# A fused attention and MLP block: GpSimd's part of the late MLP moved to VectorE, gate vectors spread over eight steps, loads and early work reordered

## The chip, the cores and the metric

The kernel runs on one core of one Trainium2 chip. The metric is the device time of one execution in microseconds (us); lower is better. Engines: PE is TensorE, DVE is VectorE, ACT is ScalarE, POOL is GpSimd, SP issues most of the DMAs. "L509" is line 509 of the kernel's source; the same statement has a slightly different line number in the two kernels.

## The reference

```python
# x: 1 x 2048 x 640; k_cache, v_cache: 1 x 32 x 2048 x 128; bf16
mod = (_silu(c) @ w_mod).reshape(c.shape[0], 6, 1, -1)      # six vectors of 640
sa, ca, ga, sb, cb, gb = ...
h = _layernorm(x) * (1 + ca) + sa
x = x + ga * (softmax(h @ wq . K / sqrt(128)) . V) @ wo      # 32 heads, cache of 2048 keys
h = _layernorm(x) * (1 + cb) + sb
# MLP: g = gelu(layernorm(h) @ w1), its four column quarters shifted by +1, -1, +2, -2 rows
#      x1 = h + shifted(g) @ w2;  y = x1 + gelu(layernorm(x1) @ w3) @ w4
x = x + gb * y
```

## The kernel before

All work is written as operations with an engine, a duration estimate and a priority. A list scheduler in the kernel's own Python (`Plan`) fixes each engine's order when the kernel is built; on the chip each engine works strictly in that order. TensorE's order follows the priorities alone. So a changed estimate or priority moves instructions without changing what is computed.

The 2048 rows go in four chunks of 512. Attention is 128 "steps" (a head and a chunk), each with eight exps of 128x1024 on ACT. The "tail" after it holds, per chunk, w1 + GELU (A), w2 (B, by tiles of 128 rows), w3 + GELU (C), w4 (D, by tiles). The letter I stands for a chunk's layernorms before A, WO for the last output projection; `WOD`, `CH` and `I3D` shift the priorities of the last output projection's drains, of the work behind B and of I3. TensorE's order of these parts is a string:

```python
TAIL = ("A0 WO B0 B1 A1 B2 B3 A2 B4 B5 B6 I3 B7 C0 D0 D1 D2 D3 C1 A3 B8 B9 B10 B11 D4 D5 D6 B12 D7 ...")
...
def ln1(ch, prio):                       # layernorm of a chunk of x, then its transpose hT
    xs = ... load_x2(...)                # DMA
    for a in (0, 2):
        for i in (a, a + 1):
            ln_stats(xs[i].ap, (xs[i],), g, i, prio)           # DVE bn_stats, bn_aggr
        rstd_act(g, a, a + 2, prio - 100)                      # ACT: Ln, then Exp(-0.5 *)
        ...                                                    # DVE normalizes, DMA transposes, DVE scales
...
MS = 17                                  # gate vectors: 8 tiles of 5 matmuls, in two steps
for n, p in enumerate((2, 4, 3, 5)):
    ...
                 MM(HD), (s_bc, W12[n % 2]), (m,), NP * (MS + i // 20) + 3 + (i % 20) * 0.34 + 0.6, accum=True)
...
def mlp_in(ch, prio):
    eng = ("POOL", "DVE" if ch == 2 else "POOL") * 2           # layernorm, scale, shift, layernorm
    ...
def w2_tile(t, key):
    ...                                                        # DVE drains PSUM, statistics, rstd_dve (10 ops of 128x2)
    for u in (t - 1, t):
        v = xb[u]
        eng, late = ("POOL", 200) if t < SQ // 128 - 4 else ("DVE", 100)
        tt(eng, v.ap, v.ap, mod_t[5][:], ALU.mult, ...)        # 128x640 f32, POOL
        tt(eng, v.ap, v.ap, x1[u].ap, ALU.add, ...)
```

## Time and profile before

| | before |
|---|---|
| median of four runs | 1432.08 us (1431.37 to 1432.74) |
| profiled span | 1424.6 us (that run took 1430.3 us) |
| end of attention (first w1 matmul) | 1223.77 us |
| last matmul ends | 1420.04 us |

The first line to look at is who holds the chain that ended last (shares of the span by engine):

```profile
PE 92%; DVE 5%; SPq 1%; DMA 1%; issue 0%; ACT 0%; POOL 0%; POOLq 0%
```

TensorE's own work holds 92% of the chain; the other 8% lie with others, and DVE has the most of that. The next three fences are timelines (start, length, engine, line, operation, count, and in brackets the idle time before with what ended it). DVE near the start:

```profile
17.86 0.49 DVE L472 BATCH_NORM_STATS2 f_small<-f_xin 128x6 f32<-128x320 bf16 x1 [6.31 <-DMA f_xin<-in_A_x_dram]
18.27 0.53 DVE L552 TENSOR_SCALAR f_hT<-f_O,f_small 128x512 bf16<-128x512 bf16 x1
```

DVE stood 6.31 us in front of a statistics operation whose x was still under way, while the hT operation behind it could have run. The second place is in the tail; POOL, then TensorE:

```profile
1279.35 6.03 POOL L508 TENSOR_TENSOR f_y<-f_y,f_mod 128x640 f32<-128x640 f32 x4 [4.07 <-ACT f_y L515]
```

```profile
1295.11 5.17 PE L884 MATMUL f_M<-f_KV,f_OO 128*128 128x320 bf16 x22 [6.41 <-DVE f_wo L888]
```

While POOL works, TensorE waits 6.41 us for a DVE that is busy with tiny operations (the prediction shows these).

### The profile page before, as it was taken

Reading aid. Unit: us, or ns where it says so; the run is one execution under the profiler, and the core shown is the slowest. Engines: PE = TensorE matmul, PEld = TensorE weight load, DVE = VectorE, ACT = ScalarE, POOL = GpSimd, SP = SyncE. Lnnn points to the kernel's source line nnn. Section 1 sums busy time; section 2 is a strip of 40 time slices with the busy share of each in tenths; the row PEclk is TensorE's granted clock in tenths of the full one; section 3 lists DMA queues with packets and bytes.
Section 4 is the critical chain, followed back from the end, with each engine's and each line's share of the span. In section 5 each row is a group of like instructions: output and inputs, shape, how many; then the busy total and the mean of one; then the engine's idle time right before and its main releaser. Section 6 shows DMA issues by size and latency. Waiting matters only on the chain.

```text
span 1424.6 us, 29987 instructions
## 1 busy us (share of the span) xinstructions
PE 1388.6 (97%) x13176; PEld 940.9 (66%) x13176; DVE 544.4 (38%) x1349; ACT 1109.6 (78%) x1180; POOL 168.4 (12%) x132
## 2 busy tenths in 40 slices
PE   8899999999999999999999999999999999888998
PEld 6566767766676766666776666776766767544554
DVE  4353332233333233333223333323333355895662
ACT  4788868888888888888888888888888888752222
POOL 0000000000000000000000000001333366463300
PEclk9999999999999999999999999999999999999999
DMA  7661632142213321241215130512262123311110
GB/s 173 133 115 21 143 101 68 35 86 53 46 35 61 79 45 35 42 97 30 50 24 97 35 52 17 100 35 55 53 117 75 16 35 76 92 38 37 33 38 23
DMA packets 258963, 88.82 MB, mean 62 GB/s; under 512 B 236625, under 2 KB 257554, under 8 KB 258834
## 3 DMA queue, kind: packets, MB, share of 16 engines
q1 hardware_dynamic: 256210, 85.41, 29.6%
q8 instruction: 104, 1.70, 0.5%
q10 hardware_dynamic: 2624, 1.51, 0.5%
q14 instruction: 25, 0.20, 0.0%
HBM read 43.48 MB, written 2.62 MB: 32 GB/s over the span
## 4 chain that ended last, share of the span: by engine, by line
PE 92%; DVE 5%; SPq 1%; DMA 1%; issue 0%; ACT 0%; POOL 0%; POOLq 0%
PE f_O L726 32%; PE f_S L707 30%; PE f_M L638 10%; PE f_M L663 9%; PE f_M L884 2%; PE f_S L884 2%; PE f_S L871 2%; PE f_O L871 2%; DMA f_xin<-in_A_x_dram 1%; DVE f_small L472 1%; PE f_S L413 1%; PE f_M L844 1%; PE f_S L844 1%; DVE f_small L492 1%; DVE f_small L493 1%; DVE f_small L491 1%
## 5 line engine op out<-in xcount | busy, mean ns | idle before, releaser
L709 ACT ACTIVATE f_PQ<-f_S 128x1024 bf16<-128x1024 f32 x1024 | 1030.6, 1022 | 174.9 <-PE f_S L707 170.9
L726 PEld LDWEIGHTS f_O<-f_KV,f_PQ 128*128 128x128 bf16 x8192 | 539.8, 98 | 214.9 <-DVE f_OO L735 4.9
L726 PE MATMUL f_O<-f_KV,f_PQ 128*128 128x129 bf16 x8192 | 613.0, 220 | 3.5 <-DVE f_OO L735 3.4
L707 PE MATMUL f_S<-f_PQ,f_KV 128*128 128x512 bf16 x2048 | 609.4, 379 | 0.9 <-ACT f_PQ L709 0.9
L671 DVE TENSOR_TENSOR f_y<-f_M,f_y 128x320 f32<-128x320 f32 x192 | 94.4, 492 | 541.0 <-PE f_M L663 541.0
L663 PE MATMUL f_M<-f_wo,f_OO 128*128 128x320 bf16 x992 | 270.2, 299 | 1.3 <-DVE f_y L669 1.3
L508 POOL TENSOR_TENSOR f_y<-f_y,f_mod 128x640 f32<-128x640 f32 x56 | 87.5, 1577 | 1138.2 <-DVE f_y L671 1065.7
L707 PEld LDWEIGHTS f_S<-f_PQ,f_KV 128*128 128x128 bf16 x2048 | 192.5, 98 | 43.1 <-ACT f_PQ L709 1.9
L638 PE MATMUL f_M<-f_hT,f_wq 128*128 128x512 bf16 x640 | 161.3, 383 | 8.3 <-DVE f_hT L552 4.2
L638 PEld LDWEIGHTS f_M<-f_hT,f_wq 128*128 128x128 bf16 x640 | 62.5, 98 | 85.2 <-DVE f_hT L559 5.5
L663 PEld LDWEIGHTS f_M<-f_wo,f_OO 128*128 128x128 bf16 x992 | 94.8, 97 | 29.5 <-DVE f_y L669 1.8
L735 DVE TENSOR_TENSOR f_OO<-f_O,f_rl 128x256 bf16<-128x256 f32 x256 | 108.4, 423 | 8.3
L641 DVE CAST f_PQ<-f_M 128x512 bf16<-128x512 f32 x128 | 88.5, 691 | 53.6 <-PE f_M L638 53.4
L733 DVE RECIPROCAL f_rl<-f_O 128x2 f32<-128x2 f32 x256 | 43.4, 170 | 48.3 <-PE f_O L726 44.1
L884 PE MATMUL f_M<-f_KV,f_OO 128*128 128x320 bf16 x252 | 41.0, 310 | 9.0 <-DVE f_wo L888 7.9
L515 ACT ACTIVATE f_xn<-f_y,f_small 128x640 bf16<-128x640 f32 x12 | 10.8, 916 | 49.0 <-DVE f_small L497 47.1
L669 DVE COPY f_y<-f_M 128x320 f32<-128x320 f32 x32 | 15.7, 490 | 70.1 <-PE f_M L663 70.1
L884 PEld LDWEIGHTS f_M<-f_KV,f_OO 128*128 128x128 bf16 x252 | 23.9, 100 | 26.4 <-DVE f_wo L888 8.5
L874 ACT ACTIVATE f_OO<-f_O 128x512 bf16<-128x512 f32 (+1 forms) x28 | 16.6, 594 | 28.3 <-PE f_O L871 28.3
L874 ACT ACTIVATE f_OO<-f_S 128x512 bf16<-128x512 f32 (+1 forms) x28 | 16.6, 594 | 18.4 <-PE f_S L871 18.4
L472 DVE BATCH_NORM_STATS2 f_small<-f_y 128x6 f32<-128x320 f32 x64 | 29.4, 478 | 1.9 <-POOL f_y L508 1.8
L884 PE MATMUL f_S<-f_KV,f_OO 128*128 128x320 bf16 x196 | 30.0, 300 | 0.0
(118 smaller groups left out, 566.5 us busy)
## 6 DMA issues: line engine op xcount, KB each, us to landing
f_KV<-in_A_v_cache_dram SPq DMA_DIRECT2D x31, 512.0 KB, 4.7
f_wo<-in_A_wo_dram SPq DMA_DIRECT2D x8, 640.0 KB, 4.2
f_xin<-in_A_x_dram SPq DMA_DIRECT2D x15, 320.0 KB, 3.8
f_wq<-in_A_wq_dram SPq DMA_DIRECT2D x7, 640.0 KB, 4.5
f_W<-in_w_mod_dram SPq DMA_DIRECT2D x4, 800.0 KB, 4.8
out_dram<-f_xin SPq DMA_DIRECT2D x16, 160.0 KB, 1.8
f_KV<-in_B_w_dram SPq DMA_DIRECT2D x5, 432.0 KB, 3.3
f_KV<-in_A_k_cache_dram SPq DMA_TRANSPOSE x128, 2.7
```

The lines of the kernel that those rows point to most:

```text
L472: P.op("DVE", lambda e, hf=hf: e.bn_stats(s[:, hf * 6:hf * 6 + 6], src[:, hf * HD:(hf + 1) * HD]), 485, src_t, (s,), prio, slack=slack)
L508: P.op(eng, lambda e: e.tensor_tensor(out=out, in0=a, in1=b, op=op), COST[eng][0], rd, wr, prio, lat=300 if eng == "POOL" else None)
L638: P.op("PE", lambda e, i=i, kk=kk: e.matmul(m.ap, wq_t[g % 2][:, kk, hh * 128:(hh + 1) * 128], hT_t[ch][:, kk, :], start=(i == 0), stop=(i ...
L641: P.op("DVE", lambda e: e.tensor_copy(q.ap, m.ap), 690, (m,), (q,), s * NP - 90)
L663: P.op("PE", lambda e, m=m, qt=qt, hf=hf, hh=hh: e.matmul(m[:, 0:HD], OT_ap[gs][:, qt, hh, :], wo_t[g % 2][:, hh, hf * HD:(hf + 1) * HD], ...
L671: P.op("DVE", lambda e, m=m, yt=yt: e.tensor_tensor(out=yt.ap, in0=m[:, 0:HD], in1=yt.ap, op=ALU.add), 490, (m, yt), (yt,), s * NP - 60)
L707: P.op("PE", lambda e, sp=sp, r=r, kt=kt: e.matmul(sp[:, r * QC:(r + 1) * QC], K_ap[b][:, kt * 128:(kt + 1) * 128], q.ap, start=True, stop ...
L709: x = P.op("ACT", lambda e, sp=sp, pt=pt: e.activation(pt.ap.rearrange("p k q -> p (k q)"), sp.ap, ACT.Exp, scale=SCALE), 1021, (sp,), (pt ...
L726: ins = e.matmul(o[bk][:, w * 129:w * 129 + 129], pt[:, r, qt * 128:(qt + 1) * 128], V_ap[b][:, u, 0:129], start=(u == 0 and w == 0), stop ...
L735: evac.append(P.op("DVE", lambda e, ov=ov, i0=i0, bk=bk: e.tensor_tensor(out=On_ap[gs][:, 2 * bk:2 * bk + 2, hh, :], in0=ov[:, 0:258].rear ...
L871: P.op("PE", lambda e, m=m, f=f, kk=kk, fs=fs: e.matmul(m[0:fs, :], w3_ap[:, kk, f * 128:f * 128 + fs], nT_ap[ch][:, kk, :], start=(kk == ...
L884: P.op("PE", lambda e, f=f, hf=hf, fs=fs: e.matmul(m[:, hf * 512:hf * 512 + HD], gT_ap[0:fs, f, i * 128:(i + 1) * 128], w4_ap[f][0:fs, hf ...
```

## The change

Its intent: DVE and POOL no longer work at the same time in the MLP; reciprocal deviations in attention need no DVE; no engine stands in front of data that a DMA has yet to bring; the gate tiles fit into TensorE's slack.

```diff
-   u.ready = max(u.ready, (o.end if o in u.deps else o.start) + u.slack)
+   u.ready = max(u.ready, (...) + u.slack + (1500.0 if o.dma and u.eng in ("DVE", "ACT") and not u.dma else 0.0))
...
-   XP, XS = (0, -195, -20, -20), (0, -1, 22, 44)          # priority of the x loads
+   XP, XS = (0, -294, -20, -20), (0, -1, 22, 44)
-               ln_stats(xs[i].ap, (xs[i],), g, i, prio)
+               ln_stats(xs[i].ap, (xs[i],), g, i, prio, 0.0 if ch == 0 else 2000.0)
-               dmaT(... (raw[i],), prio)                  # transposes of a chunk
+               dmaT(... (raw[i],), prio - 400)
...                                                        # K, V and wq loads: other priorities
-   ... NP * (MS + i // 20) + 3 + (i % 20) * 0.34 + 0.6    # gate tiles: two steps
+   ... NP * (MS + i // KT) + 4 + i % KT + 0.65            # one tile in each of eight steps
...
-   WOD, CH, I3D = -50, -100, 50
+   WOD, CH, I3D = 0, -200, -200                           # and a new TAIL, which starts
+   # "A0 WO B0 B1 B2 A1 B3 A2 B4 B5 B6 B7 C0 I3 D0 D1 D2 D3 C1 A3 B8 ... D4 D5 D6 D7 B12 ..."
-   eng = ("POOL", "DVE" if ch == 2 else "POOL") * 2
+   eng = "DVE" if tail else "POOL"                        # POOL only for the first three chunks
-       shift(g, a, a + 2, prio)                           # DVE
+       negate(g, a, a + 2, prio, 1200.0)                  # ACT, in the first three chunks
-   (w2_tile: POOL multiply and add per tile)
+   (w4_tile: DVE adds w2's result to PSUM, multiplies by the gate, adds x1; last two tiles as before)
```

`rstd_dve` also loses one of its operations (the shift and the multiply become one). The 1500 and the 2000 are allowances in ns: the scheduler takes data that a DMA brings to be ready so much later (the 1500 for every DVE or ACT operation behind a DMA, the 2000 for the later chunks' statistics). POOL keeps the layernorms of the first three chunks; in the changed kernel its last operation ends at 1227.5 us, 21 us after the end of attention.

More of the change, by code (lines that the diff above doesn't have):

```diff
@@ L148, in schedule @@
                 u.ndep -= 1
-                u.ready = max(u.ready, (o.end if o in u.deps else o.start) + u.slack)
+                u.ready = max(u.ready, (o.end if o in u.deps else o.start) + u.slack + (1500.0 if o.dma and u.eng in ("DVE", "ACT") and not u.dma else 0.0))
                 if u.ndep == 0:
@@ L353, in fast_path @@
     xn = [T(t[:]) for t in xn_t]
-    tmp = [T(t[:]) for t in tmp_t] + [T(flat(wo_t[1])[:, i * 2 * D:(i + 1) * 2 * D].bitcast(F32)) for i in range(2)]
+    tmp = [T(t[:]) for t in tmp_t]
     rl = T(rl_t[:])
@@ L459, in fast_path @@
     nm = [T() for _ in range(NMV)]
-    nw = [[T(small(4)) for _ in range(4)] for _ in range(4)]
+    nw = [[T(small(4)) for _ in range(2)] for _ in range(4)]
     n_mv, n_nw = [0], [0]
@@ L481, in rstd_dve @@
         r = rs_ap[g][:, a:b]
-        v_, i_, t_, _u = nw[n_nw[0] % 4]
+        v_, t_ = nw[n_nw[0] % 4]
         n_nw[0] += 1
         n = b - a
-        v, it, t = v_[:, 0:n], i_[:, 0:n].bitcast(I32), t_[:, 0:n]
+        v, t = v_[:, 0:n], t_[:, 0:n]
         D_ = lambda f, rd, wr: P.op("DVE", f, 170, rd, wr, prio)
         D_(lambda e: e.tensor_scalar_add(out=v, in0=mv_ap[g][:, a:b, 1], scalar1=EPS), tuple(mvs[g][a:b]), (v_,))
-        D_(lambda e: e.tensor_scalar(out=it, in0=v.bitcast(I32), scalar1=1, scalar2=None, op0=ALU.logical_shift_right), (v_,), (i_,))
-        D_(lambda e: e.tensor_scalar(out=r.bitcast(I32), in0=it, scalar1=-1.0, scalar2=1595932665.0, op0=ALU.mult, op1=ALU.add), (i_,), (rs[g],))
+        D_(lambda e: e.tensor_scalar(out=r.bitcast(I32), in0=v.bitcast(I32), scalar1=-0.5, scalar2=1595932665.0, op0=ALU.mult, op1=ALU.add), (v_,), (rs[g],))
         for ca, cb in ((-0.703952253, 1.68191391), (-0.5, 1.5)):
@@ L498, in shift, with negate @@
                                                      op0=ALU.mult, op1=ALU.mult), 170, tuple(mvs[g][a:b]) + (rs[g],), (nm[g],), prio)
+    def negate(g, a, b, prio, slack):
+        P.op("ACT", lambda e: e.activation(nm_ap[g][:, a:b], mv_ap[g][:, a:b, 0], ACT.Copy, scale=-1.0), 220, tuple(mvs[g][a:b]), (nm[g],), prio, slack=slack)
     def normed(dst, dst_t, src, src_t, g, i, fp, prio):
@@ L503, in normed @@
              430 if fp else 240, (src_t, mvs[g][i], rs[g]), (dst_t,), prio)
-    COST = {"POOL": (1600, 1300), "DVE": (825, 430)}
+    COST = {"POOL": (1600, 950), "DVE": (825, 430)}
     def tt(eng, out, a, b, op, rd, wr, prio):
@@ L510, in scaled @@
     def scaled(eng, out, out_t, src, src_t, g, i, prio):
-        r, n = rs_ap[g][:, i:i + 1], nm_ap[g][:, i:i + 1]
-        rd = (src_t, rs[g], nm[g])
+        r, n, mu = rs_ap[g][:, i:i + 1], nm_ap[g][:, i:i + 1], mv_ap[g][:, i, 0:1]
         if eng == "ACT":
-            P.op("ACT", lambda e: e.activation(out, src, ACT.Identity, scale=r, bias=n), act(D), rd, (out_t,), prio)
-        else:
-            P.op(eng, lambda e: e.tensor_scalar(out=out, in0=src, scalar1=r, scalar2=n, op0=ALU.mult, op1=ALU.add), COST[eng][1], rd, (out_t,), prio,
-                 lat=300 if eng == "POOL" else None)
-    XP, XS = (0, -195, -20, -20), (0, -1, 22, 44)
+            P.op("ACT", lambda e: e.activation(out, src, ACT.Identity, scale=r, bias=n), act(D), (src_t, rs[g], nm[g]), (out_t,), prio)
+        elif eng == "POOL":
+            P.op("POOL", lambda e: e.tensor_scalar(out=out, in0=src, scalar1=n, scalar2=r, op0=ALU.add, op1=ALU.mult), COST[eng][1],
+                 (src_t, rs[g], nm[g]), (out_t,), prio, lat=300)
+        else:
+            P.op("DVE", lambda e: e.tensor_scalar(out=out, in0=src, scalar1=mu, scalar2=r, op0=ALU.subtract, op1=ALU.mult), COST[eng][1],
+                 (src_t, rs[g], mvs[g][i]), (out_t,), prio)
+    XP, XS = (0, -294, -20, -20), (0, -1, 22, 44)
     def ln1(ch, prio):
@@ L556, in ln1 @@
             for i in range(4):
-                dmaT(lambda e, i=i: e.dma_start_transpose(hT_t[ch][:, :, i * 128:(i + 1) * 128], xn[i].ap), 160, (xn[i],), (raw[i],), prio)
+                dmaT(lambda e, i=i: e.dma_start_transpose(hT_t[ch][:, :, i * 128:(i + 1) * 128], xn[i].ap), 160, (xn[i],), (raw[i],), prio - 400)
             for k in range(KT):
@@ L591, in load_head @@
         first = step_of(h // HG, 0, h % HG)
-        pr = (first - 12) * NP if h >= HG else -200 + 20 * h
-        n = max(0, first * NP - 12) if h < HG else (first - 12) * NP
+        pr = (first - 12) * NP if h >= HG else -310 + 20 * h
+        n = first * NP - 14 if h < HG else (first - 12) * NP
         load_k(h, pr, need=from_slot(n))
-        load_v(h, pr + 1, need=from_slot(n + 2))
+        load_v(h, pr + 1, need=from_slot(n + 1))
     def load_group(g):
@@ L600, in load_group @@
         load_wo(g, (step_of(g, 0, 0) - 2) * NP, from_slot((step_of(g, 0, 0) + 1) * NP + 12 * (g == 0)))
-    load_wq(0, 1, HG, -190)
+    load_wq(0, 1, HG, -295)
     for h in range(1, NKV):
@@ L611, in fast_path @@
         dma("SP", lambda e, n=n, p=p: e.dma_start(w_half[n % 2], w_mod[:, p * D:(p + 1) * D].rearrange("(k p) n -> p k n", p=128)),
-            800, (), (W12[n % 2],) + (tuple(wm) if n < 2 else ()), MS * NP - 30 + n, from_slot(MS * NP - 20 + 3 * n))
+            800, (), (W12[n % 2],) + (tuple(wm) if n < 2 else ()), MS * NP - 30 + n, from_slot((MS + 2 * n) * NP - 20))
         for hf in range(2):
@@ L618, in fast_path @@
                 P.op("PE", lambda e, m=m, sl=sl, k=k, n=n: e.matmul(m[:, 0:HD], s_bc[:, k, :], w_half[n % 2][:, k, sl], start=(k == 0), stop=(k == KT - 1)),
-                     MM(HD), (s_bc, W12[n % 2]), (m,), NP * (MS + i // 20) + 3 + (i % 20) * 0.34 + 0.6, accum=True)
+                     MM(HD), (s_bc, W12[n % 2]), (m,), NP * (MS + i // KT) + 4 + i % KT + 0.65, accum=True)
             P.op("DVE", lambda e, m=m, p=p, hf=hf: e.tensor_scalar_add(out=mod[p][hf].ap, in0=m[:, 0:HD], scalar1=1.0 if p == 4 else 0.0),
                  490, (m,), (mod[p][hf],), NP * MS - 60)
-    TAIL = ("A0 WO B0 B1 A1 B2 B3 A2 B4 B5 B6 I3 B7 C0 D0 D1 D2 D3 C1 A3 B8 B9 B10 B11 D4 D5 D6 B12 D7 B13 B14 C2 B15 "
+    TAIL = ("A0 WO B0 B1 B2 A1 B3 A2 B4 B5 B6 B7 C0 I3 D0 D1 D2 D3 C1 A3 B8 B9 B10 B11 D4 D5 D6 D7 B12 B13 B14 B15 C2 "
             "D8 D9 D10 D11 C3 D12 D13 D14 D15").split()
     WOKEY = 3000 + 50 * TAIL.index("WO")
-    WOD, CH, I3D = -50, -100, 50
+    WOD, CH, I3D = 0, -200, -200
     evac = []
@@ L676, in wo_group @@
                 if hf:
-                    tt("DVE" if last and qt % 2 else "POOL", x1[t].ap, w.ap, xb[t].ap, ALU.add, (w, xb[t]), (x1[t],) + tuple(hT[ch]), WOKEY + WOD if last else s * NP)
+                    tt("DVE" if last else "POOL", x1[t].ap, w.ap, xb[t].ap, ALU.add, (w, xb[t]), (x1[t],) + tuple(hT[ch]), WOKEY + WOD if last else s * NP)
                 if s == NS - 1 - HG and i == 7:
@@ L750, in rstd @@
                 rstd_dve(g, a, a + 2, prio)
+                shift(g, a, a + 2, prio)
             else:
                 rstd_act(g, a, a + 2, prio, 1200.0)
-            shift(g, a, a + 2, prio)
+                negate(g, a, a + 2, prio, 1200.0)
         for a in (0, 2):
@@ L762, in mlp_in @@
                 b = xb[t]
-                scaled("ACT" if tail else eng[i], b.ap, b, x1[t].ap, x1[t], g1, i, prio)
-                tt(eng[i], b.ap, b.ap, mod_t[4][:], ALU.mult, (b,) + tuple(mod[4]), (b,), prio)
-                tt(eng[i], b.ap, b.ap, mod_t[3][:], ALU.add, (b,) + tuple(mod[3]), (b,), prio)
+                scaled("ACT" if tail else eng, b.ap, b, x1[t].ap, x1[t], g1, i, prio)
+                tt(eng, b.ap, b.ap, mod_t[4][:], ALU.mult, (b,) + tuple(mod[4]), (b,), prio)
+                tt(eng, b.ap, b.ap, mod_t[3][:], ALU.add, (b,) + tuple(mod[3]), (b,), prio)
                 ln_stats(b.ap, (b,), g2, i, prio, 500.0)
@@ L769, in mlp_in @@
                 t = ch * 4 + i
-                scaled("ACT" if tail else eng[i], xn[i].ap, xn[i], xb[t].ap, xb[t], g2, i, prio)
+                scaled("ACT" if tail else eng, xn[i].ap, xn[i], xb[t].ap, xb[t], g2, i, prio)
                 dmaT(lambda e, i=i: e.dma_start_transpose(nT_ap[ch][:, :, i * 128:(i + 1) * 128], xn[i].ap), 160,
@@ L859, in w2_tile @@
                 dmaT(lambda e, j=j, z=z: e.dma_start_transpose(nT_ap[ch][:, :, j * 128:(j + 1) * 128], z.ap), 160, (z,), (nT[ch][j],), key + CH)
-            for u in (t - 1, t):
-                v = xb[u]
-                eng, late = ("POOL", 200) if t < SQ // 128 - 4 else ("DVE", 100)
-                tt(eng, v.ap, v.ap, mod_t[5][:], ALU.mult, (v,) + tuple(mod[5]), (v,), key + late)
-                tt(eng, v.ap, v.ap, x1[u].ap, ALU.add, (v, x1[u]), (v,), key + late)
+            if t == SQ // 128 - 1:
+                for v in (xb[t - 1], xb[t]):
+                    u = t - 1 if v is xb[t - 1] else t
+                    tt("DVE", v.ap, v.ap, mod_t[5][:], ALU.mult, (v,) + tuple(mod[5]), (v,), key + 100)
+                    tt("DVE", v.ap, v.ap, x1[u].ap, ALU.add, (v, x1[u]), (v,), key + 100)
     def w3_part(ch, key):
@@ L878, in w4_tile @@
         i = t % 4
-        w, b = tmp[2 + t % 2], xb[t]
+        b = xb[t]
         m = Tile(pool="W")
@@ L887, in w4_tile @@
         o_ = xin[t % 4]
-        P.op("DVE", lambda e: e.tensor_tensor(out=two(w.ap), in0=wide(m), in1=two(mod_t[5][:]), op=ALU.mult), 825, (m,) + tuple(mod[5]), (w,) + ((wo[1],) if t < 2 else ()), key - 1000)
-        P.op("DVE", lambda e: e.tensor_tensor(out=o_.ap, in0=w.ap, in1=b.ap, op=ALU.add), 825, (w, b), (o_,), key)
+        if t < SQ // 128 - 2:
+            P.op("DVE", lambda e: e.tensor_tensor(out=two(b.ap), in0=wide(m), in1=two(b.ap), op=ALU.add), 825, (m, b), (b,), key - 1000)
+            tt("DVE", b.ap, b.ap, mod_t[5][:], ALU.mult, (b,) + tuple(mod[5]), (b,), key)
+            tt("DVE", o_.ap, b.ap, x1[t].ap, ALU.add, (b, x1[t]), (o_,), key)
+        else:
+            w = tmp[t % 2]
+            P.op("DVE", lambda e: e.tensor_tensor(out=two(w.ap), in0=wide(m), in1=two(mod_t[5][:]), op=ALU.mult), 825, (m,) + tuple(mod[5]), (w,), key - 1000)
+            tt("DVE", o_.ap, w.ap, b.ap, ALU.add, (w, b), (o_,), key)
         dma("SP", lambda e: e.dma_start(out2d[t * 128:(t + 1) * 128, :], o_.ap), 160, (o_,), (), key)
```

## The prediction

> **What bounds the kernel now.** I read the page first (busy shares, then the chain of work that ended last), then a table of windows, then the list of waits of TensorE, then the timeline around each gap. The page's first part:
>
> ```profile
> PE 1388.6 (97%) x13176; PEld 940.9 (66%) x13176; DVE 544.4 (38%) x1349; ACT 1109.6 (78%) x1180; POOL 168.4 (12%) x132
> ```
>
> TensorE (PE) is busy for 97% of the 1424.6 us span and the chain puts 92% of the span on it, so little is to be had outside its gaps. The windows show where they lie; the columns are window and width, then PE, weight load, DVE, ACT and POOL busy, granted clock, DMA share, GB/s.
>
> ```profile
> 0.00:30.00 30.00, 24.12 (x313) 19.18 (x314) 14.49 (x44) 10.91 (x20) 1.15 (x12) 0.94 0.72 174
> 50.00:100.00 50.00, 44.83 (x434) 29.96 (x435) 26.07 (x77) 37.59 (x47) 0.00 (x0) 0.97 0.58 117
> 400.00:600.00 200.00, 200.00 (x2018) 140.23 (x2016) 60.73 (x149) 174.83 (x174) 0.00 (x0) 1.00 0.26 49
> 1250.00:1300.00 50.00, 39.18 (x202) 20.00 (x200) 47.68 (x113) 20.01 (x31) 35.05 (x24) 0.90 0.20 37
> ```
>
> The middle of attention is solid: one head step takes 9.26 us of matmuls (8.17 us without output projection, which is eight exps of 1022 ns). The gaps are at the start, before 100 us, and around 1250 to 1300 us, where DVE is 95% busy and POOL 70%. Part of "busy" at the start is dummy matmuls that keep the clock up. TensorE's waits:
>
> ```profile
> PE f_M L884 <- DVE f_wo L888: 7.9, 2, 6.4
> PE f_M L638 <- DVE f_hT L552: 4.2, 1, 4.2
> PE f_M L638 <- DVE f_hT L559: 4.0, 1, 4.0
> PE f_O L726 <- DVE f_OO L735: 3.4, 3, 1.7
> PE f_M L844 <- DVE f_y L847: 2.4, 1, 2.4
> PE f_M L618 <- DVE f_mod L620: 2.1, 4, 0.6
> ```
>
> All are waits on DVE. The longest is this stretch of DVE's timeline (start, length, operation):
>
> ```profile
> 1282.44 1.47 DVE L489 TENSOR_SCALAR f_small<-f_small 128x2 int32<-128x2 int32 x1
> 1283.94 1.45 DVE L491 SCALAR_TENSOR_TENSOR f_small<-f_small 128x2 f32<-128x2 f32 x1
> 1285.42 1.32 DVE L492 TENSOR_TENSOR f_small<-f_small 128x2 f32<-128x2 f32 x1
> ```
>
> These are reciprocal-square-root steps on 128x2 elements; at 1277 us the same lines take 0.16 us. POOL runs 1.5 us tensor_tensors back to back from 1279.35 to 1295.4: each small DVE operation lasts as long as one of them. Ten in a row hold the PSUM drain L888 back to 1294.25, and the matmuls of the third output tile start at 1295.11.
>
> **What the Trainium skill says.** "GPSIMD Engine Reference", section 8 Key points: GpSimd "Shares its SBUF interfaces with VectorE — contention with DVE instructions in a 2-port perf mode or with two SBUF inputs." The trace agrees, 1.3 to 1.5 us against 0.16. "TensorE: Matmul & The Clock Gate", What's actually happening: an idle array falls to half clock after about 3.4 us and needs such a time of work to recover. The trace agrees in kind: after the 6.41 us wait 28 matmuls take 6.09 us, not 4.29; after the 2.44 us wait ten take 2.73, not 1.52, so a shorter gap can do it too. "ScalarE: Activation LUTs", What ACT_TABLE_LOAD costs: about 1283 ns plus a drain of about 1380 per switch. The trace has 1283 ns; with the small operation between two loads a round trip took 1231.63 to 1236.86.
>
> **The change part by part.** TensorE's mathematics stays the same; what I count is its gaps, each in the coordinates of the trace before.
>
> *Start: +5.3 us.* DVE stands idle from 11.5 to 17.86 because the next chunk's statistics, which await a DMA, stand in front of the three operations that make the first hT. Their inputs, the transposes, are ready at 14.1 (ACT did its two at 14.14). In the new order those operations come first. DVE then makes hT at 14.14, 14.6 and 15.1 (0.45 apart); the projection ends near 16.1 with a warm array, the copy (0.69) at 16.8, scores, and the first exp at 17.5 instead of 22.77. The first K lands near 16.2 (last issue near 9, 7.2 to land), in time.
>
> *Second chunk: +4.8.* The wait at 48.4 cost 3.95 plus slow clock. The step from one projection's end (41.89) to the next (55.46) took 13.57 against 8.17, so 5.4, and the following one 0.5 more: 5.9. It came from the hT transposes standing behind K loads in SP's queue. They now come ahead. But DVE now awaits them before it drains the second head: x landing near 22.3, normalised near 28.7, transposes issued 27.4 to 32.6, last landing about 35.4 (4.1 each), five operations 1.7, to 37.1; TensorE wants that output bank at about 37.0 and gets its halves at 37.8 and 38.4. I leave 1.1 as a new stall.
>
> *Fourth chunk: +2.7.* At 80.5 to 92.4 a step took 11.84 against 9.26, because statistics awaiting x stood before drains. The new order puts them behind the projection copy, and x is asked for earlier relative to use.
>
> *Gate vectors: +3.1.* Two steps took 13.56 each, 8.6 over normal, of which 40 matmuls of 0.135 are 5.4; the rest is waiting for a PSUM bank. One tile in each of eight steps gives 8 x 0.68, the same 5.4, and a whole step to drain.
>
> *Tail: +15.2 on paper.* From 1223.77 to 1420.0 is 196.3 us. The work in it is 20 x 1.08 (w1) + 4.3 (last output projection) + 16 x 1.36 (w2) + 56 x 1.08 (w3) + 16 x 4.22 (w4) = 175.5. So 20.8 are gaps and slow clock, plus 2.8 just before. POOL is out of the MLP; DVE gets 14 x 3 + 2 x 4 = 50 tile operations of 0.82 instead of 16 x 2 + 4 x 2 = 40, 8 us more over the tail, but loses some 26 us of stretched small ones. Walking the new order by hand:
> - Attention ends at 1222.0, 1.7 earlier (no 4.1 us pair of contended DVE operations before the drains).
> - ACT now switches tables twice in the tail, seven loads there (with the GELU's first) against four: 3 x 1.28 = 3.9 us, and the first trip lies inside the GELUs of the first w1 part. With four PSUM tiles TensorE stands from 1227.4 to 1230.75; the output projection ends at 1235.9, as before (1235.7).
> - The second trip delays the next GELUs; the w2 tile that needs them starts at 1247.5, against 1245.7.
> - Then the 2.44 wait shrinks to 0.4, w3 starts at 1260.2 against 1262.2, the w4 tiles at 1275.5 against 1278.5.
> - From there DVE has slack (drain of the first w4 tile at 1280, needed 1284.2), so the 6.41 + 1.8, the 1.53 and the small ACT waits vanish. 129.2 us of matmuls end at 1404.8 against 1420.0.
>
> From the 15.2 I take 2.0 for half clock after the two new waits on ACT (3.3 and 2.0 us) and 2.5 for waits my hand walk misses, leaving 10.7. The moved negation adds 12 ACT operations of 0.2 us inside ACT's slack of 1.08 us per step: nothing.
>
> Sum: 5.3 + 4.8 + 2.7 + 3.1 + 10.7 = 26.6, and 1431.9 - 26.6 = 1405.3. The deduction is the doubtful part: without the 2.5 it would be 1402.8. I put the point between, at 1404.
>
> **Rivals.**
> 1. *ACT's table switches take the place of the POOL contention.* For: three more loads, in front of GELUs that TensorE needs at once, while DVE waits in order behind POOL results that themselves await ACT. Against: it is one stretch of 25 us and later work has slack. If each trip costs 4 us more than my walk says, about 1412.
> 2. *DVE becomes the bound after 1250.* For: 50 tile operations and all statistics on one engine, 95% busy there before. Against: that business is mostly stretched waiting; each w4 tile gives DVE 4.22 us for three operations (2.5). If w4 tiles wait 1 us on average for half of them, 1412.
> 3. *The reordered loads only move the stall.* DMA is at 0.9 from 3 to 18 us, and three more K transposes go before x. If x lands at 25 instead of 22.3, the second query copy and the second head's drain are late by 2 to 3 us each: 1408.
> 4. *Everything hides.* Neither new stall nor half clock: 15.2 in the tail, 1.1 back at the second chunk: 1431.9 - 32.2 = 1399.7.
>
> **Range and chances.** Faster by 2% means below 1403.2, right beside my point. The surest parts (start 5.3, gates 3.1, the 6.41 us wait with its slow clock 8.2) make 16.6 us, so 1415 is a pessimistic end and I set 1413; the low end is below rival 4 by some 3 us. Slower would need a new wait of 55 us: hardly. Faster by over 2% 0.46, within 0.53, slower 0.01.
>
> **What would show it right or wrong.** First exp near 17.5; no wait of TensorE for hT of several us before 60 us; eight steps near 9.94 us around 190 to 260 us and no wait for f_mod; no 128x2 DVE operation above 0.5 us after POOL's last operation near 1233; seven table loads in the tail, a wait of TensorE on ACT of about 3 us some 5 us after attention's end; at most 0.5 us of waits per w4 tile. It is wrong if TensorE still waits several us on DVE after 1250 us with POOL silent, or if a head step in mid attention is not 9.26 us.

## The result, and the profile after

| | before | after |
|---|---|---|
| median | 1432.08 us | 1400.81 us (1400.64 to 1401.11) |
| ratio of fast runs | | 0.9782 (95%: 0.9765 to 0.9799) |
| profiled span | 1424.6 us | 1395.0 us |

A ratio is the mean time of one kernel's fast runs over that of the other's of the same rounds, so it is not quite the ratio of the medians quoted. All runs compared here are in the fast state. The changed kernel is faster by 2.2%. The profiled run of before was 1.8 us quicker than its median, so the traces explain 29.6 of the 31.3 us.

The page's busy line and its chain line, after:

```profile
PE 1380.7 (99%) x13176; PEld 939.8 (67%) x13176; DVE 518.0 (37%) x1337; ACT 1114.6 (80%) x1195; POOL 123.5 (9%) x106
```

```profile
PE 96%; ACT 2%; POOL 1%; DVE 0%; DMA 0%; issue 0%; ACTq 0%; POOLq 0%
```

The matmuls are the same; DVE's 5% of the chain became 0, ACT has 2% now. The windows that the prediction showed (columns as there):

```profile
0.00:30.00 30.00, 26.01 (x344) 20.39 (x345) 15.85 (x48) 14.18 (x23) 1.15 (x12) 1.00 1.03 219
50.00:100.00 50.00, 50.00 (x506) 34.71 (x503) 25.54 (x75) 45.18 (x53) 0.00 (x0) 1.00 0.58 109
1250.00:1300.00 50.00, 50.00 (x269) 25.34 (x268) 23.16 (x71) 26.04 (x42) 0.00 (x0) 1.00 0.17 40
```

TensorE fills both later windows. In the last one DVE went from 47.68 to 23.16 us busy although it has more full-size operations to do over the tail (78 of 128x640 with two inputs after the end of attention, 59 before): much of the rest had been waiting. TensorE's waits, all of 1 us and more:

```profile
PE f_S L668 <- ACT f_PQ L836: 3.2, 1, 3.2
PE f_S L712 <- ACT f_PQ L714: 2.7, 3, 1.8
PE f_S L850 <- ACT f_PQ L836: 1.7, 1, 1.7
PE f_S L413 <- POOL f_ones L381: 1.0, 1, 1.0
```

No wait for DVE above 0.3 us is left. The first and the third are new: TensorE waits for GELUs (L836) in the tail. The second has a piece at the start. ACT, then TensorE:

```profile
24.34 0.20 ACT L477 ACTIVATE f_small<-f_small 128x2 f32<-128x2 f32 x1 [2.03 <-DVE f_small L473]
```

```profile
25.50 0.60 PE L712 MATMUL f_S<-f_PQ,f_KV 128*128 128x512 bf16 x2 [1.83 <-ACT f_PQ L714]
```

ACT stood before an Ln whose statistics DVE could not finish before the second chunk's x had landed (20.9 us), and the exps behind the Ln, which TensorE needed, stood with it.

Where the 29.6 us came from, by the starts of the query projections (one per step) in both traces:

| stretch | before | after | gained |
|---|---|---|---|
| to the third projection | 32.47 | 29.04 | 3.4 |
| to the sixth (second chunk's first stall lies between) | 63.09 | 53.56 | 9.5, 6.1 more |
| to the ninth (fourth chunk) | 92.36 | 80.51 | 11.8, 2.3 more |
| to the twenty-eighth (gate tiles) | 276.90 | 261.90 | 15.0, 3.2 more |
| to the end of attention | 1223.77 | 1206.27 | 17.5, 2.5 more |
| from there to the end of the last matmul | 196.3 | 184.2 | 12.0 more |

Between the twenty-eighth and the 118th projection nothing changed (15.0 at both ends). The last 2.5 us of attention were two waits of TensorE for DVE (1.66 and 0.90 us at 1217 and 1218 us), which are gone.

### The profile page after: what moved, and what is told of

It reads as the page before. It is cut to its first block, busy times and chain, and to the rows that moved or that the text cites. A ratio compares the mean times of both kernels' runs of the same rounds, so it can differ in the third digit from the quotient of the medians.

```text
span 1395.0 us, 29964 instructions
## 1 busy us (share of the span) xinstructions
PE 1380.7 (99%) x13176; PEld 939.8 (67%) x13176; DVE 518.0 (37%) x1337; ACT 1114.6 (80%) x1195; POOL 123.5 (9%) x106
## 3 DMA queue, kind: packets, MB, share of 16 engines
q10 hardware_dynamic: 2624, 1.51, 0.5%
## 4 chain that ended last, share of the span: by engine, by line
PE 96%; ACT 2%; POOL 1%; DVE 0%; DMA 0%; issue 0%; ACTq 0%; POOLq 0%
PE f_O L731 33%; PE f_S L712 31%; PE f_M L643 10%; PE f_M L668 10%; PE f_S L890 2%; PE f_M L890 2%; PE f_S L877 2%; PE f_O L877 2%; ACT f_PQ L836 1%; PE f_S L413 1%; PE f_S L850 1%; PE f_M L850 1%; POOL f_y L511 0%; PE f_S L832 0%; PE f_M L623 0%; DMA f_xin<-in_A_x_dram 0%
## 5 line engine op out<-in xcount | busy, mean ns | idle before, releaser
L511 POOL TENSOR_TENSOR f_y<-f_y,f_mod 128x640 f32<-128x640 f32 x40 | 61.3, 1542 | 1058.2 <-DVE f_y L676 1050.8
L890 PE MATMUL f_S<-f_KV,f_OO 128*128 128x320 bf16 x224 | 34.3, 300 | 0.0
L890 PE MATMUL f_M<-f_KV,f_OO 128*128 128x320 bf16 x224 | 34.3, 300 | 0.0
L472 DVE BATCH_NORM_STATS2 f_small<-f_y 128x6 f32<-128x320 f32 x64 | 29.3, 478 | 10.7 <-POOL f_y L511 10.7
L890 PEld LDWEIGHTS f_M<-f_KV,f_OO 128*128 128x128 bf16 x224 | 20.6, 97 | 14.0 <-issue 5.5
L890 PEld LDWEIGHTS f_S<-f_KV,f_OO 128*128 128x128 bf16 x224 | 20.5, 97 | 13.3 <-issue 4.2
```

The source lines that it names most:

```text
L511: P.op(eng, lambda e: e.tensor_tensor(out=out, in0=a, in1=b, op=op), COST[eng][0], rd, wr, prio, lat=300 if eng == "POOL" else None)
L890: P.op("PE", lambda e, f=f, hf=hf, fs=fs: e.matmul(m[:, hf * 512:hf * 512 + HD], gT_ap[0:fs, f, i * 128:(i + 1) * 128], w4_ap[f][0:fs, hf ...
```

## The experiments

Twelve kernels ran. The first three do one part of the change alone, on the kernel before.

**Gate vectors alone** (b_gates): the two gate lines of the diff, nothing else.

> The kernel before with only the gate vectors spread, one tile in each of eight steps. Theory (the parts of the gain are separate and add up): eight steps of 9.94 us take the place of two of 13.56 us and six of 9.26 us, so 3.1 to 3.2 us less than before, about 1428.9 us, and no wait of TensorE for the gate tile. Rival (the steps saved are given back in the attention that follows, because the exponentials set its pace): 1431 to 1432 us.

Measured: 1428.58 us against 1431.72 us, ratio 0.998 (0.9972 to 0.9987). The steps are 9.94 us long and the wait for the gate tile is gone. 3.1 us, as the theory has it.

**Loads and allowances alone** (b_loads): the lines of the diff down to the loads.

> The kernel before with only the reordered loads and the two allowances for data that arrives by DMA. Theory (all that was gained in the first nine steps comes from here): the start of the ninth step (the step after the eighth chunk-head pair) moves from 92.4 to 80.5 us and stays so to the end, about 1420 us. Rival (part of the early gain comes from VectorE having less to do, which is in the other part): 1423 us or more.

Measured: 1419.01 us against 1431.72, ratio 0.9912 (0.9894 to 0.993). The ninth projection starts at 80.39 us. 12.7 us: the last projection starts 12.0 us earlier than before (1192.89 us for 1204.87). The theory holds for the first nine steps, but "stays so to the end" hides two things that cancel in part. The last step of attention became about 1.5 us longer (the granted clock was 0.50 from 1207.54 to 1210.95 us). And the tail became about 3.2 us shorter, 193.1 us for 196.3: in this run DVE's order in the tail differs from that of the kernel before, and TensorE's waits fell elsewhere. (The first matmul of the tail has no record in this trace; its start is worked out from the matmul before it.)

**MLP part alone** (b_mlp): all the rest of the diff.

> The kernel before with only the MLP part: its elementwise work on VectorE and ScalarE, the shorter chain of small operations, the new order of the tail. Theory (the parts add up): the last step of the attention 2.7 us shorter and the tail 12.1 us shorter, so about 14.8 us less in the profile and 1415 to 1418 us. Rival (the tail gained because it found other clock or other loads than before): 1420 us or more, with waits for VectorE left in the tail.

Measured: 1415.90 us against 1431.72, ratio 0.9889 (0.9872 to 0.9906). TensorE's waits in it:

```profile
PE f_M L643 <- DVE f_hT L557: 4.7, 1, 4.7
PE f_M L643 <- DVE f_hT L564: 4.4, 1, 4.4
PE f_S L668 <- ACT f_PQ L836: 3.2, 1, 3.2
```

The two early waits for hT are those of the kernel before; the tail is that of the changed kernel, with its new wait for a GELU. 3.1 + 12.7 + 15.8 = 31.6 us, and the whole change gained 31.3. The parts add up, though they are not wholly separate, since the loads' part moves the tail by some us.

**The allowances taken out again** (a_noslack): in the changed kernel, without the 1500 and the 2000.

```diff
-   ... + u.slack + (1500.0 if o.dma and u.eng in ("DVE", "ACT") and not u.dma else 0.0))
+   ... + u.slack)
-               ln_stats(xs[i].ap, (xs[i],), g, i, prio, 0.0 if ch == 0 else 2000.0)
+               ln_stats(xs[i].ap, (xs[i],), g, i, prio)
```

> The changed kernel with the two allowances for data that arrives by DMA taken out again; priorities and order of the loads stay. VectorE then has the second chunk's statistics, whose x landed at 20.9 us, ahead of the drain of the first head's queries (15.75 us in the changed kernel). Theory (the early start comes from these allowances): the first scores come at about 22.5 us in place of 16.5 us, the later steps as in the changed kernel, and the time is 1404 to 1407 us. Rival (the order of the loads alone makes the early start): 1400 to 1402 us.

Measured: 1408.92 us, ratio to before 0.984: 8.1 us more than the changed kernel, above the range of the theory.

```profile
22.82 1.89 PE L712 MATMUL f_S<-f_PQ,f_KV 128*128 128x512 bf16 x4 [6.09 <-DVE f_PQ L646]
```

The first scores come at 22.82 us, as expected. What the theory missed: the eighth step took 11.23 us again in place of 9.26 (projections at 78.02 and 89.25), so the fourth chunk's gain came from the allowances too, about 2 us. The second chunk's stall did not come back (8.18 us from the fourth to the fifth projection): that one was cured by the order of the loads.

**Needless GpSimd work in the tail** (a_noise). Nobody reads its result; the other engines' order is the same.

```diff
+    for n in range(44):
+        P.op("POOL", lambda e: e.tensor_tensor(out=mod_t[2][:], in0=mod_t[2][:], in1=mod_t[3][:], op=ALU.add), ...)
```

> The changed kernel with 44 needless GpSimd additions of 128x640 after GpSimd's last useful instruction, some 68 us of them, read by nobody; the instruction order of the other engines is the same. Theory (GpSimd beside VectorE costs, whatever GpSimd computes): the 128x2 operations of VectorE in that stretch rise from 0.15 us to about 1.3 us each, TensorE waits for VectorE again, and the time is 1406 to 1415 us. Rival (the tail gained by the new order and the shorter chain alone): under 1403 us, small operations still under 0.3 us.

Measured: 1436.51 us, ratio 1.0024 (1.0014 to 1.0033): all of the gain and 4 us more are lost. This is DVE in the window 1231 to 1290 us, grouped by line and form (busy time and mean ns behind the bar), first in the changed kernel, then with the needless work:

```profile
L511 DVE TENSOR_TENSOR f_y<-f_y,f_mod 128x640 f32<-128x640 f32 x12 | 9.6, 818 | 0.0
L491 DVE TENSOR_TENSOR f_small<-f_small 128x2 f32<-128x2 f32 x15 | 2.1, 155 | 0.0
L472 DVE BATCH_NORM_STATS2 f_small<-f_y 128x6 f32<-128x320 f32 x18 | 8.2, 478 | 0.0
L853 DVE TENSOR_TENSOR f_y<-f_S,f_y 128x640 f32<-128x640 f32 x3 | 2.5, 825 | 1.5 <-PE f_S L850 1.4
```

```profile
L491 DVE TENSOR_TENSOR f_small<-f_small 128x2 f32<-128x2 f32 x9 | 10.3, 1150 | 0.0
L511 DVE TENSOR_TENSOR f_y<-f_y,f_mod 128x640 f32<-128x640 f32 x4 | 7.1, 1778 | 0.0
L472 DVE BATCH_NORM_STATS2 f_small<-f_y 128x6 f32<-128x320 f32 x14 | 6.5, 474 | 0.0
L853 DVE TENSOR_TENSOR f_y<-f_S,f_y 128x640 f32<-128x640 f32 x3 | 2.4, 810 | 0.2 <-PE f_S L850 0.2
```

The orders of TensorE, DVE and ACT are the same in both traces. A 128x2 multiplication goes from 155 to 1150 ns, a 128x640 one from 818 to 1778. Statistics (one source) and the drain of a PSUM tile (L853: one source in PSUM, one in SBUF) do not change. Operations `tensor_scalar` with one source are held too: of 128x2 from 163 to 990 ns (L487) and, on integers, from 158 to 582 (L488), of 128x640 from 607 to 1154 (L522). The Trainium skill, "SBUF — State Buffer", section Who interferes with whom, says just this: a VectorE instruction with two SBUF inputs contends with a GpSimd instruction that reads SBUF, the winner holds the shared port for its whole instruction, and the other fully blocks; one SBUF input outside the 2-port modes does not contend. The trace agrees, line by line; for `tensor_scalar` the page leaves the 2-port modes as the reason, which no run here shows by itself. TensorE's longest wait is then

```profile
PE f_M L850 <- DVE f_y L853: 14.4, 1, 14.4
```

because the drain, itself not slowed, stands behind slowed operations. The theory's mechanism holds; its size (5 to 14 us) was far too small for 76 us of unbroken GpSimd work.

**The same time of GpSimd in shorter instructions** (a_noise_ts): 78 operations `tensor_scalar` (one source) in place of the 44 additions.

> As the run with 44 needless GpSimd additions, but 78 GpSimd operations of one source (tensor by two scalars, 128x640, 0.87 us each), about the same 68 us of GpSimd. Theory (a VectorE instruction that meets a GpSimd instruction ends when that one ends, whatever its form): small operations of 0.4 to 0.9 us in place of 0.15, and 1410 to 1425 us. Rival (only GpSimd instructions with two sources hold VectorE): small operations of 0.15 us and under 1403 us.

Measured: 1409.78 us, ratio 0.9846 (0.9831 to 0.9861).

```profile
L491 DVE TENSOR_TENSOR f_small<-f_small 128x2 f32<-128x2 f32 x14 | 6.8, 503 | 0.0
```

GpSimd was busy for 72.6 us here against 75.8 us in the run before, 0.93 us per instruction against 1.72, and the loss is 9.0 us against 35.7. A GpSimd instruction with one source also holds VectorE; the time fell just short of the theory's range. The loss fell fourfold for instructions little more than half as long, which no proportion explains; the two runs differ in form as well as in length, so what share each has is not settled.

**The old order of the tail** (a_oldorder): the changed kernel with `TAIL` and `WOD, CH, I3D` of the kernel before.

> The changed kernel with the order of the tail and the three priorities of the kernel before; engines and chain as in the changed kernel. Theory (taking GpSimd out of the MLP is what gains, not the order): 1400 to 1404 us. Rival (the order does most of it): 1408 us or more.

Measured: 1407.64 us, ratio 0.9833 (0.9818 to 0.9848): 6.8 us more, near the rival. The theory as I had put it falls. The traces show why. TensorE, then ACT:

```profile
1235.28 1.87 PE L850 MATMUL f_S<-f_W,f_PQ 128*128 128x320 bf16 x10 [4.31 <-ACT f_PQ L836]
```

```profile
1225.95 1.28 ACT L477 ACT_TABLE_LOAD   x1
1227.56 1.28 ACT L478 ACT_TABLE_LOAD   x1
1229.07 1.28 ACT L836 ACT_TABLE_LOAD   x1
```

In this order a round trip through three activation tables stands between the first GELU of the second chunk and the others, and TensorE waits 4.31 us for them in place of 1.7. The split is clean when the second w4 tile's start is the mark:

| us | end of attention to second w4 tile | from there to last matmul's end |
|---|---|---|
| before | 60.6 | 135.6 |
| changed, old order | 65.1 | 125.7 |
| changed | 58.6 | 125.7 |

The second stretch gains 10 us whatever the order: GpSimd is silent there in both changed kernels. In the first, the changed engines lose 4.5 us with the old order, and the new order wins that back and 2 more. So in these three traces taking GpSimd out gains after the first w4 tile, and the order is there to hide what the table loads cost before it. The mark is not a firm border, though: b_loads, with GpSimd still at work, has about 65.0 and 128.1 us there, so the cost of the contention moves with the timing. Over the whole tail the old order leaves 5.5 of the 12.0 us (196.3, 190.8, 184.2), and about 2.3 against the 193.1 us of b_loads. The new order with the kernel before's engines was not run, so what the order does alone stays open.

**Deviations after attention on DVE** (a_rstd). Two of the third chunk's Ln and Exp fall after attention; here DVE's chain replaces them.

```diff
-            if tail:
+            if tail or (second and ch == NC - 2):
                 rstd_dve(g, a, a + 2, prio)
...                                                        # and a negation on DVE beside it
```

> The changed kernel, but the second reciprocal deviation of the third chunk, which falls after the attention, is computed on VectorE with the chain of small operations in place of Ln and Exp on ScalarE. Theory (the table loads that Ln and Exp bring into the tail hold the GELUs, and with them TensorE): one table load is left after the attention in place of seven, the waits of 3.2 and 1.7 us of TensorE for the GELU disappear, the slow matmuls behind them too, and the time is 1394 to 1397 us. Rival (the chain on VectorE, beside GpSimd's last multiplications and additions, stretches to over 1 us for each small operation and the third chunk comes late): the waits move to the third chunk's first matmuls and the time stays at 1399 to 1403 us.

Measured: 1400.01 us, ratio 0.9771 (0.9754 to 0.9787): no gain. One table load is left and the wait of 3.2 us is gone, but, DVE and TensorE:

```profile
1208.48 1.53 DVE L488 TENSOR_SCALAR f_small<-f_small 128x2 int32<-128x2 int32 x1
```

```profile
1227.14 4.02 PE L832 MATMUL f_O<-f_wo,f_W 128*128 128x512 bf16 x10 [1.89 <-ACT f_PQ L836]
```

The first of the two chains meets GpSimd's last multiplications (three of its operations took 0.72, 1.53 and 0.98 us), the second hardly does, and TensorE waits in other places. The rival has the time right. Its mechanism is shown in part only: the waits (0.69 and 1.89 us, followed by half clock) came in the second chunk's w1, not at the third chunk's first matmuls, and a_best300 below shows late drains behind them.

**Ln and Exp of the second chunk later** (a_start): the scheduler lets ACT take the exps first.

```diff
-            rstd_act(g, a, a + 2, prio - 100)
+            rstd_act(g, a, a + 2, prio - 100, 2500.0 if ch == 1 else 0.0)
```

> The changed kernel, but the schedule puts Ln and Exp of the second chunk some exponentials later on ScalarE. Theory (ScalarE, which works in order, stood 2.03 us at 22.3 us for statistics of x whose load had landed at 20.9 us, and TensorE 1.83 us for it): the wait of 1.83 us is gone, the transposes of the second chunk still come in time, and the time is 1.5 to 2 us less, 1398.8 to 1399.4 us. Rival (the second chunk comes later by as much and the wait moves to its first projection): the same time as the changed kernel, 1400.8 us, with a wait for the second chunk's hT at 45 us.

Measured: 1399.36 us (1398.56 to 1400.39), ratio 0.9773 (0.9759 to 0.9786). The wait of 1.83 us is gone and the third projection starts at 27.03 us in place of 29.04; 0.6 us of that is given back by the sixth (52.12 for 53.56), with a wait of 0.41 us for the drain of a query tile, none for the second chunk's hT. The size, 1.4 us, is at the edge of what the theory said. The intervals of the two ratios overlap, so the trace and not the time decides this one.

**a_start, a_rstd and the last w_o tiles drained early** (a_best300; `WOD = -300`).

> The changed kernel with three edits: the later Ln and Exp of the second chunk, the third chunk's last reciprocal deviations on VectorE, and the w_o tiles of the tail drained ahead of VectorE's other work. Theory (with the deviations on VectorE the gain was eaten because the last w_o tiles were drained 5 us late and held the PSUM banks that the w1 tiles wait for): with both, TensorE's waits of 3.2, 1.9 and 1.7 us in the tail go and 1.8 us at the start, so 1393 to 1396 us. Rival (the GELUs themselves are the limit of that stretch): 1397.5 to 1399.5 us, the start's gain alone.

Measured: 1397.87 us, ratio 0.9763 (0.9749 to 0.9776): the rival's number, 1.5 us under a_start. The wait of 1.7 us for the GELU stays, and a new one of 1.2 us, for the third chunk's transposed tile, is there. My reason for a_rstd's failure (banks held by late drains) explained a part: its waits of 0.69 and 1.89 us and the slow matmuls behind them are gone, and the tail is 1.7 us shorter than a_rstd's.

**With the third chunk's normalizing on ACT and A1 one tile earlier** (a_best3).

```diff
-   TAIL = ("A0 WO B0 B1 B2 A1 B3 A2 ...
+   TAIL = ("A0 WO B0 B1 A1 B2 B3 A2 ...
-   scaled("ACT" if tail else eng, xn[i].ap, ...)
+   scaled("ACT" if ch >= NC - 2 else eng, xn[i].ap, ..., 3000.0 if ch == NC - 2 and a == 0 else 0.0)
```

> The changed kernel with the later Ln and Exp of the second chunk, the third chunk's last deviations on VectorE, its last normalizing on ScalarE (idle for 9.75 us there) in place of GpSimd, the w_o tiles drained early, and the second chunk's w1 tiles one w2 tile pair earlier in TensorE's order. Theory (what was left in the version before it were two waits, 1.7 us for the second chunk's GELUs and 1.2 us for the third chunk's transposed tile): both go, 1394 to 1396 us. Rival (these waits only move on to the next tile, because VectorE's chain is no faster): 1397 to 1399 us.

Measured: 1398.10 us, ratio 0.9765 (0.9752 to 0.9778). The waits (2.1 and 1.1 us) are still there, and the time is the rival's; its reason, that DVE's chain is no faster, is not shown by itself.

**One table for Ln and Exp** (a_preload2): a_start, with the set that holds both functions loaded by name ahead of each of the two late Ln.

```diff
+    def ln_op(e, g, a, b, pre):
+        if pre:
+            e.preload_act_table_set(EXPSET)                # "natural_log_exp_and_others"
+        return e.activation(rs_ap[g][:, a:b], mv_ap[g][:, a:b, 1], ACT.Ln, bias=EPS)
```

> The changed kernel with the later Ln and Exp of the second chunk (1399.4 us by itself, with the waits of 3.2 and 1.7 us in the tail as before) and one thing more: ahead of each of the two Ln that fall after the attention, the table set that holds both Ln and Exp is loaded explicitly, so that Exp loads none. Nothing else moves on any engine. Theory (each table load ahead of the GELUs that TensorE waits for costs its 1.28 us once): five table loads after the attention in place of seven, the wait of 3.2 us falls to about 1.9 us, the one of 1.7 us stays, and the time is 1397 to 1398.5 us. Rival (the load is hidden behind other waits, or the set is loaded again for Exp): 1399 to 1400 us.

Measured: 1397.32 us (1396.65 to 1398.51), ratio 0.9752 (0.9736 to 0.9768), as the theory has it. TensorE in the changed kernel, then ACT and TensorE in this one:

```profile
1215.04 0.75 PE L668 MATMUL f_S<-f_wo,f_OO 128*128 128x320 bf16 x4 [3.22 <-ACT f_PQ L836]
1217.22 2.12 PE L668 MATMUL f_S<-f_wo,f_OO 128*128 128x320 bf16 x8
```

```profile
1208.40 1.28 ACT L477 ACT_TABLE_LOAD   x1
1209.93 0.20 ACT L483 ACTIVATE f_small<-f_small 128x2 f32<-128x2 f32 x1
```

```profile
1212.79 0.70 PE L673 MATMUL f_S<-f_wo,f_OO 128*128 128x320 bf16 x4 [1.86 <-ACT f_PQ L841]
```

The Exp (L483) follows without a load of its own; the wait fell from 3.22 to 1.86 us, by about one load (1.28 us). Twelve matmuls soon after it (the eight shown and the four before them) took 2.99 us in the changed kernel, from start to start, most of it at a granted clock of 0.50 (1215.56 to 1218.97 us); here they took 1.78 us at 1.00. That makes 1.36 + 1.21 = 2.6 us in the two traces, against the changed kernel; by the medians, against a_start, it is 2.0. The wait of 1.7 us stays because of where its load stands: in the changed kernel the Ln's load of the second trip ran at 1217.98 us, while ACT waited for DVE's statistics until 1223.88; here the load named ahead of the Ln stands behind that wait (1220.41 us, after 4.70 us idle). From the end of the wait to the first GELU it is 3.05 us here and 3.12 there. This version beats both kernels, the changed one by 3.5 us; against a_best300 (0.55 us) it can't be told apart.

## Why the prediction was right or wrong

The time, 1400.81 us, lies in the range and 3.2 us under the point of 1404. The verdict "faster by over 2%" had been given 0.46.

- **Start (+5.3).** The mechanism was right and so was the first exp (17.14 us for 17.5). But only 3.4 us were left by the third projection: ACT's Ln stood before the exps (2.03 us) and TensorE lost 1.83 us. I had followed DVE's queue and not ACT's. a_start shows it by taking it away.
- **Second chunk (+4.8).** 6.1 us. The new stall of 1.1 us that I had left for it did not come: the transposes landed at about 34.2 us, not 35.4, so the drain behind them at 36.75 us was not late.
- **Fourth chunk (+2.7).** 2.3 us by the ledger (the prediction's own 11.84 and 9.26 give 2.6, not 2.7). a_noslack shows that the allowance did it, as I had put it.
- **Gate vectors (+3.1).** 3.2 us, eight steps of 9.94 us; b_gates alone 3.1.
- **Tail (+15.2 on paper, +10.7 kept).** This is the step that failed, and only in its size: 2.5 + 12.0 = 14.5 us came. The walk's marks were close: the wait of 3.3 us was 3.2; the second trip's w2 tile came 26.4 us after the end of attention (walked: 25.5), w3 39.0 (38.2), the first w4 tile 54.4 (53.5). I then took off 2.0 us for half clock, and it was 1.2; and 2.5 us for waits that the walk misses, and after the first w4 tile there was none at all. Of the 4.5 us that I took off, 3.8 were not needed (14.5 less 10.7).
- **Rivals.** The first (table switches in the place of contention) is real: 3.2 and 1.7 us, seven loads as predicted. The new order kept it small; with the old one the second trip cost 4.3 us in one wait. The second (DVE as the new bound) did not happen: 23 us busy in 50. My count for it was too low all the same: without the w2 drains DVE has 62 tile operations after attention in place of 43, not 50 in place of 40, because the last chunk's layernorms and two more additions moved to it as well. The third (the stall only moves) did not happen. The fourth (everything hides, 1399.7) came nearest.
- **The check list** held: no DVE operation of 128x2 above 0.5 us after POOL's last (0.15 us on average), no wait in the w4 tiles, 9.26 us in mid attention, seven table loads. That ACT might hold up the start was not on it.

## What to carry to other kernels

Look for the engine that waits in order in front of something that is not there yet (here a DMA's data, twice); an operation moved back a few places costs nothing and was worth about 8 us (a_noslack). When two engines share a port, moving work to the "idle" one can cost more than it frees: a chain of tiny operations is hit hardest, since each can wait for a whole instruction of the other. And before you move work to ACT, count the table loads that it brings and where in the order they fall.

## What the Trainium skill lacked or had wrong

- "ScalarE: Activation LUTs". Section Table sets: "ln(x) then exp(x)" is said to need one load, since one set has both. In the changed kernel's tail Ln and Exp each brought a load (seven in all with the GELUs'); only when the set was loaded by name ahead of Ln did Exp do without (five, and 2.0 us less). The page names the set but does not say that the automatic choice may pick two. Section What ACT_TABLE_LOAD costs: the 1283 ns agree (1.28 us), but the drain of about 1380 ns is not in these traces: in a_preload2, with a load at 1208.40 us, the Ln started at 1209.70 us, and in a_oldorder the three loads of a round trip started 1.61 and 1.51 us apart with the small operations in between (1225.95, 1227.56, 1229.07 us).
- "SBUF — State Buffer", Who interferes with whom, has the lock that the runs show, but not how far the cost depends on the kind of GpSimd's instructions: 76 us of two-source pieces of 1.72 us cost 35.7 us, and 73 us of one-source pieces of 0.93 us cost 9.0 us. Which of the two differences does it is open.
- No page gives a length below the 3.4 us from which on slow matmuls may follow a wait. In the kernel before one of 2.44 us was followed by slow matmuls (ten in 2.73 us for 1.52), in a_preload2 one of 1.86 us was not. Nor does the length of the wait alone decide: after the same wait of 3.2 us the clock was 0.50 for 3.41 us in the changed kernel and for 6.82 us in a_start.
